# Loading and turning batch 0 by units of 192 tokens in a windowed attention with a gated feed-forward

## The chip, the cores and the metric

The kernel runs on one core of a Trainium2 chip. The metric is the device time of one execution in microseconds; the median of three runs before the change is 339.5 us (339.3 to 340.37). The core has a matrix engine (TensorE, PE in the profile; its weight loads are PEld), a vector engine (VectorE, DVE), a scalar engine (ScalarE, ACT), GpSimd (POOL) and SyncE (SP), which issues transfers. Transfers that change the type from float32 to float16 are issued from GpSimd here, plain ones from SyncE.

## What is computed

Causal attention with a window of 64 tokens over 8 batches, 8 heads, 576 tokens and 64 elements per head, then a gated feed-forward layer over the 4608 tokens.

```python
scores = q @ k.T / sqrt(64)                  # (8, 8, 576, 576)
mask = (rel >= 0) & (rel < 64)               # rel = query position - key position
attn = softmax(where(mask, scores, -1e9))
x = (attn @ v).transpose(0, 2, 1, 3).reshape(4608, 512)
out = (maximum(x @ w_gate, 0) * (x @ w_val)) @ w_out      # 512 -> 1536 -> 512
```

All inputs and the output are float32. The kernel calculates its matrix products in float16 with float32 sums.

## The kernel before

The attention works in 24 units of 192 tokens, three to a batch (U = 192, UB = 3). Two units make one tile of 384 tokens (TT) for the feed-forward layer, which has 12 tiles. The program is written as an interleaving: a small planner with a clock ("W") is given pieces of attention at planned times, and they are put into the instruction streams between the matmuls of the feed-forward layer. The clock orders the instructions; it makes no engine wait.

For a batch, k and q arrive with 18 tokens to a partition, four heads over 128 partitions, and VectorE turns them in blocks of 32, so that the head's elements lie on the partitions (32 partitions per head, two elements of float16 packed as one float32):

```python
def qk_load(b, name, hh):                    # from GpSimd, float32 -> float16
    tile_ = nat[b, name, hh] = a_in.tile([128, S // 32 * D], FP16, ...)
    src = (q if name == "q" else k)[b, G * hh:G * hh + G]
    nc.gpsimd.dma_start(tile_, src.rearrange("h (i j) d -> (h i) (j d)", i=32))

def k_first(hh):                             # batch 0 only: float32, from SyncE
    k32 = nat["k32", hh] = x_sb.tile([128, S // 32 * D], FP32, ...)
    nc.sync.dma_start(k32, k[0, G * hh:G * hh + G].rearrange(...))

def qk_trans(b, name, hh, j0=0, j1=S // 32):
    ...
    nc.vector.transpose(dst.rearrange("p (i j) -> p j i", i=32)[:, j0:j1], src[:, j0:j1])
```

A unit's values stand in a tile of 128 keys for each of its three windows of 64 queries. The upper 64 partitions are loaded, and the lower ones are copied from the upper ones of the window before by VectorE:

```python
def v_load(u):
    for w in range(UB):
        nc.gpsimd.dma_start(v16s[uu][64:128, w, :, 0:64], ...)

def v_low(u):
    if uu > 0:
        nc.vector.tensor_copy(v16s[uu][0:64, 0, :, 0:64], v16s[uu - 1][64:128, UB - 1, :, 0:64])
    nc.vector.tensor_copy(v16s[uu][0:64, 1:UB, :, 0:64], v16s[uu][64:128, 0:UB - 1, :, 0:64])
```

A unit then runs: scores (`u_st`, 48 matmuls with 32 rows each), exp on ScalarE (`u_exp`), mask by a product on VectorE (`u_mask`; units 0 and 1 instead add a bias before the scores by a matmul with the identity, `u_bias`), values and row sums (`u_pv`), copies of the values out of PSUM on ScalarE (`u_copy`), the row sums turned (`u_sum`), their reciprocal turned back (`u_back`) and the product (`u_norm`), which writes the tile `xt`. Units 0 and 1 have narrow value matmuls with the sums made by separate matmuls with ones; from unit 2 on a wide form gives values and sums at once, for which `v16s` holds columns of ones. `heat` is a row of matmuls on zeros, which do no part of the result.

The feed-forward layer takes a tile or a half of one (`hidden`: for each block of w_gate and w_val four matmuls, relu on ScalarE, gate product on VectorE) and then `output` with w_out. The start of the program, cut:

```python
for hh in range(2):
    k_first(hh)
for hh in range(2):
    qk_load(0, "q", hh)
...
heat(12, units[0]["st"][1][3])
bands(); constants(); v_ones(1, nc.vector)
for hh in range(2):
    for part in range(2):
        k_round(hh, part, 2)                 # float32 -> float16 on ScalarE
W.at(5.5, lambda: v_load(0)); W.at(5.6, lambda: v_load(1))
W.at(6.4, lambda: w_load(*G3[0], 13.7))      # w_gate, first third
W.at(6.5, lambda: w_load(*V3[0], 16.3))      # w_val, first third
...
W.at(21.0, lambda: v_ones(2, nc.vector)); W.at(21.0, lambda: v_ones(0, nc.vector))
plan_unit(2, 23.0, ...)
plan_unit(3, 42.15, *fast)
plan_unit(4, 49.3)
plan_unit(5, 56.95, *fast)
T = 67.0
...
W.advance(13.7)
ready(1)
hidden(0, 0, U, 0, 4, 4)                     # unit 0, first four blocks
ready(2)
hidden(0, U, TT, 0, 4, 4)                    # unit 1, first four blocks
hidden(0, 0, TT, 4, NF, 4)
output_by_rows(0)
ready(3)
hidden(1, 0, U)
output(1, (0,))
ready(4)
hidden(1, U, TT)
output(1, (1, 2))
for t in range(2, NU // 2):
    ready(2 * t + 2)
    hidden(t, 0, TT)
    (output if t < NU // 2 - 1 else output_last)(t)
```

`ready(n)` puts attention into the streams until n units are done; `w_load` loads a third of a weight matrix (512 KB as float16) from GpSimd. In the profile L419 is the gate and value matmul of `hidden`, L433 the output matmul, L407 the gate product, L356 `u_norm`, L311 the wide values, L289 and L296 the narrow values and sums, L249 the scores, L198 and L199 `v_low`.

Of the kernel before, what the change touches and what calls it, by code (L numbers as in the profile page):

```python
# [12 lines left out]
MUL = mybir.AluOpType.mult  # L13

# [28 lines left out]
def kernel(  # L43
# [10 lines left out]
    nc = tc.nc  # L54
# [32 lines left out]
    v16s = [persist.tile([128, UB, H, 128], FP16, name=f"v16_{i}") for i in range(UB)]  # L87
# [4 lines left out]
    ident = consts.tile([128, 128], FP16)  # L92

# [21 lines left out]
    def v_ones(i, eng):  # L115
        eng.memset(v16s[i][64 if i == 0 else 0:, 0, :, 64:128], 1.0)
        for w in range(1, UB):
            eng.memset(v16s[i][:, w, :, 64:128], 1.0)  # L118

    def k_zeros():  # L120
        nc.vector.memset(kTs[1][:, :, 0:64], 0.0)

    def constants():
        nc.vector.memset(kTs[0][:, :, 0:64], 0.0)
        nc.vector.memset(v16s[0][0:64, 0], 0.0)
        nc.vector.memset(ones, 1.0)
        nc.vector.memset(ones0, 1.0)
        nc.vector.memset(ones0[0:64], 0.0)

# [40 lines left out]
    def k_first(hh):  # L170

        k32 = nat["k32", hh] = x_sb.tile([128, S // 32 * D], FP32, name="k32", bufs=2)
        nc.sync.dma_start(k32, k[0, G * hh:G * hh + G].rearrange("h (i j) d -> (h i) (j d)", i=32))

    def k_round(hh, part, parts):
        n = S // 32 * D // parts
        if part == 0:
            nat[0, "k", hh] = a_in.tile([128, S // 32 * D], FP16, name=f"k{hh}", bufs=2)
        nc.scalar.copy(nat[0, "k", hh][:, n * part:n * part + n], nat["k32", hh][:, n * part:n * part + n])  # L179
# [8 lines left out]
    def v_load(u):  # L188
        b, uu = divmod(u, UB)
        for w in range(UB):  # L190
            k0 = U * uu + 64 * w
            nc.gpsimd.dma_start(v16s[uu][64:128, w, :, 0:64], v[b, :, k0:k0 + 64].rearrange("h p d -> p h d"))  # L192

    def v_low(u):

        uu = u % UB
        if uu > 0:
            nc.vector.tensor_copy(v16s[uu][0:64, 0, :, 0:64], v16s[uu - 1][64:128, UB - 1, :, 0:64])  # L198
        nc.vector.tensor_copy(v16s[uu][0:64, 1:UB, :, 0:64], v16s[uu][64:128, 0:UB - 1, :, 0:64])  # L199

    def u_bias(u, gs=range(G)):

        d = units.setdefault(u, {})
        if "st" not in d:
            st_tiles(u)
        d["biased"] = True
        for to in d["st"][0] + d["st"][1] if u == 0 else [d["st"][0][g] for g in gs]:
            n = 1 if u == 0 else 2
            nc.tensor.matmul(to[:, 0:n * U].rearrange("p (n c) -> p n c", c=64), ident,
                             bias[:, None, :].to_broadcast([128, n * UB, 64]),  # L210
                             start=True, stop=False, skip_group_check=True)
# [6 lines left out]
    def st_tiles(u):  # L218
        d = units.setdefault(u, {})
        one = lambda name: f_ps.tile([128, 512], FP32, name=name, tag="h")  # L220
        two = lambda name: a_ps.tile([128, 2, 512], FP32, name=name, tag="a")
        if u == 0:
            d["st"] = [[one("st") for _ in range(G)]]
            halves = [two("st") for _ in range(2)]
            d["st"].append([halves[g // 2][:, g % 2] for g in range(G)])
        elif u == 1:
            half = two("st")
            d["st"] = [[half[:, 0], half[:, 1], one("st"), one("st")]] * 2
        else:
            halves = [two("st") for _ in range(2)]  # L230
            d["st"] = [[halves[g // 2][:, g % 2] for g in range(G)]] * 2
        if u == 0:
            d["spare"] = d["st"][1][3][:, 256:512]
            d["st"] = [[x[:, 0:512 if hh == 1 and g == 3 else 256] for g, x in enumerate(row)] for hh, row in enumerate(d["st"])]

    def u_st(u, hhs=(0, 1)):
        d = units.setdefault(u, {})
        kT, qT = kTs[(u // UB) % 2], qTs[(u // UB) % 2]
        biased = "biased" in d
        if not biased:  # L240
            st_tiles(u)
        ks = U * (u % UB)
        for hh in hhs:
            for w in range(UB):
                c = U * (hh if u else 0) + 64 * w
                for dh in range(2):
                    for g in range(G):
                        rows = slice(32 * g, 32 * g + 32)
                        nc.tensor.matmul(  # L249
                            d["st"][hh][g][:, c:c + 64],  # L250
                            kT[rows, hh, ks + 64 * w:ks + 64 * w + 128, dh],
                            qT[rows, hh, ks + 64 * w:ks + 64 * w + 64, dh],
                            start=(dh == 0 and not biased), stop=(dh == 1),
                            skip_group_check=biased)
        d.setdefault("p", [None] * G)
        return 0.49

    def u_exp(u, g, hh=None):
        d = units[u]
        if not hh:  # L260
            d["p"][g] = a_p.tile([128, 2, U], FP16, name="p")
        if hh is None:
            nc.scalar.activation(d["p"][g].rearrange("p h c -> p (h c)"), d["st"][0][g][:, 0:2 * U], ACT.Exp, scale=scale)  # L263
        else:
            nc.scalar.activation(d["p"][g][:, hh], d["st"][hh][g][:, 0:U], ACT.Exp, scale=scale)
# [6 lines left out]
    def u_pv(u, cs=(0, 2, 1, 3)):  # L272
        if u > 1:
            return u_pv_wide(u)
        d = units[u]
        v16 = v16s[u % UB]
        if u == 0 and cs[0] == 0:
# [348 lines left out]
```

The softmax here doesn't subtract the row's maximum and nothing guards it: scores larger than these inputs give would overflow.

## Time and profile before

| | before |
|---|---|
| median of three runs | 339.5 us (339.3 to 340.37) |
| span of the profiled run | 337.9 us |
| TensorE busy | 325.5 us, 96% |
| VectorE busy | 260.3 us, 77% |
| ScalarE busy | 176.7 us, 52% |
| GpSimd busy, load issues included | 74.0 us, 22% |

A line of the timeline gives the start, the busy time, the engine, the line of the kernel, the operation, output and inputs with their shapes, how many instructions are merged in it, and in square brackets the idle time before it with what ended it. Busy time of TensorE includes `heat`, so the share at the start says nothing of useful work.

### The profile page before, as it was taken

How to read it: one execution, taken by the hardware profiler on the slowest of the kernel's cores; microseconds unless marked ns; L12 is line 12 of the kernel's file. 1: busy time of each engine (PE TensorE's matmuls, PEld its weight loads, DVE VectorE, ACT ScalarE, POOL GpSimd, SP SyncE). 2: the span in 40 equal slices, each digit the busy share in tenths (PEclk: the TensorE clock that was granted, in tenths of full speed). 3: DMA queues.
4: the chain of work that ended last, by engine and by line, in shares of the span. 5: the costliest groups of instructions: out<-in, count | busy, mean ns of one | idle time of the engine just before them, and what ended most of it. 6: DMA issues, size and time to landing. Idle time of an engine off the chain costs nothing.

```text
span 337.9 us, 8605 instructions
## 1 busy us (share of the span) xinstructions
PE 325.5 (96%) x3522; PEld 197.3 (58%) x3522; DVE 260.3 (77%) x493; ACT 176.7 (52%) x383; POOL 74.0 (22%) x121
## 2 busy tenths in 40 slices
PE   8699998999999999999999999999999999999995
PEld 4485485856546656655655655654655664664653
DVE  5878878998998874897989974888889874884430
ACT  4546165745636646645555564564564664653321
POOL 8724341250213221320210410150120200000000
PEclk9989999999999999999999999999999999999999
DMA  8999998496343933491242853296214402001002
GB/s 214 178 206 193 204 203 135 31 139 98 24 77 49 158 51 71 29 185 70 17 53 73 111 75 98 18 143 123 17 10 111 32 3 93 2 2 71 24 0 94
DMA packets 52886, 29.44 MB, mean 87 GB/s; under 512 B 39280, under 2 KB 44272, under 8 KB 52848
## 3 DMA queue, kind: packets, MB, share of 16 engines
q0 software_dynamic: 47088, 18.29, 47.4%
q1 hardware_dynamic: 5616, 10.55, 8.7%
q8 instruction: 27, 0.44, 0.6%
q14 instruction: 11, 0.09, 0.1%
q10 hardware_dynamic: 144, 0.07, 0.1%
HBM read 37.75 MB, written 9.44 MB: 140 GB/s over the span
## 4 chain that ended last, share of the span: by engine, by line
PE 81%; DVE 13%; issue 3%; DMA 2%; ACT 0%; DVEq 0%; ACTq 0%; POOLq 0%
PE h L419 52%; PE op L433 21%; PE pv L311 5%; PE st L249 3%; DVE sT L341 2%; DVE qT L186 2%; DMA q<-in_q_dram 2%; DVE g_sb L407 2%; DVE kT L186 1%; DVE xt L356 1%; DVE rs L350 1%; DVE p L270 1%; PE op L465 1%; DVE v L118 1%; DVE rT L348 0%
## 5 line engine op out<-in xcount | busy, mean ns | idle before, releaser
L419 PE MATMUL h<-xt,wg 128*128 128x384 f16 (+1 forms) x640 | 117.5, 313 | 1.7 <-DVE xt L356 1.7
L419 PE MATMUL h<-xt,wv 128*128 128x384 f16 (+1 forms) x640 | 116.7, 311 | 1.0 <-DVE g_sb L407 1.0
L407 DVE TENSOR_TENSOR g_sb<-r_sb,h 128x384 f16<-128x384 f32 x144 | 78.3, 550 | 48.8 <-PE h L419 47.1
L404 ACT ACTIVATE r_sb<-h 128x384 f32<-128x384 f32 x144 | 70.2, 492 | 67.0 <-PE h L419 55.3
L433 PE MATMUL op<-wo,g_sb 128*128 128x512 f16 x420 | 93.0, 379 | 0.0
L192 POOL DMA_DIRECT2D v<-in_v_dram x72 | 49.5, 696 | 181.0 <-PE pv L311 95.3
L419 PEld LDWEIGHTS <-wg 128*128 128x128 f16 x640 | 61.5, 99 | 36.5 <-DVE xt L356 1.6
L419 PEld LDWEIGHTS <-wv 128*128 128x128 f16 x640 | 59.0, 98 | 31.7 <-issue 1.3
L433 PEld LDWEIGHTS <-g_sb 128*128 128x128 f16 x420 | 40.3, 98 | 46.6
L341 DVE STREAM_TRANSPOSE sT<-pv 64x384 f32<-64x384 f32 x88 | 51.1, 580 | 9.7 <-PE pv L311 7.7
L329 ACT COPY xv<-pv 64x384 f32<-64x384 f32 x88 | 41.6, 473 | 21.5 <-DVE sT L341 8.1
L440 ACT COPY o_sb<-op 128x512 f32<-128x512 f32 x35 | 20.5, 586 | 54.6 <-PE op L433 54.6
L263 ACT ACTIVATE p<-st 128x384 f16<-128x384 f32 x92 | 39.7, 492 | 4.2 <-PE st L249 4.1
L270 DVE TENSOR_TENSOR p<-p,mask 128x384 f16<-128x384 f16 x88 | 27.5, 352 | 0.3 <-ACT p L263 0.2
L350 DVE STREAM_TRANSPOSE rs<-rT 128x768 f32<-128x768 f32 x24 | 23.5, 978 | 0.8
L356 DVE TENSOR_TENSOR xt<-xv,rs 128x768 f16<-128x768 f32 x24 | 22.8, 948 | 0.8
L311 PEld LDWEIGHTS <-v 128*128 128x128 f16 x528 | 18.6, 98 | 4.2 <-issue 0.8
L186 DVE STREAM_TRANSPOSE kT<-k 128x576 f32<-128x576 f32 (+1 forms) x18 | 19.7, 1121 | 1.4 <-ACT k L179 1.3
L311 PE MATMUL pv<-p,v 128*128 128x64 f16 x528 | 19.7, 193 | 1.1 <-DVE p L270 0.6
L186 DVE STREAM_TRANSPOSE qT<-q 128x576 f32<-128x576 f32 x16 | 18.9, 1239 | 1.1 <-DMA q<-in_q_dram 1.1
L249 PEld LDWEIGHTS <-kT 32*128 32x128 f16 x1152 | 11.0, 92 | 10.0 <-issue 9.9
L249 PE MATMUL st<-qT,kT 32*128 32x64 f16 x1152 | 13.9, 189 | 2.3 <-DVE qT L186 2.0
(47 smaller groups left out, 91.8 us busy)
## 6 DMA issues: line engine op xcount, KB each, us to landing
out_dram<-o_sb SPq DMA_DIRECT2D x35, 256.0 KB, 2.0
q<-in_q_dram POOLq DMA_DIRECT2D x16, 288.0 KB, 8.1
v<-in_v_dram POOLq DMA_DIRECT2D x72, 64.0 KB, 3.2
k<-in_k_dram POOLq DMA_DIRECT2D x14, 288.0 KB, 6.1
wg<-in_moe_w_gate_dram POOLq DMA_DIRECT2D x3, 512.0 KB, 10.1
wv<-in_moe_w_val_dram POOLq DMA_DIRECT2D x3, 512.0 KB, 11.9
wo<-in_moe_w_out_dram POOLq DMA_DIRECT2D x3, 512.0 KB, 13.7
k<-in_k_dram SPq DMA_DIRECT2D x2, 576.0 KB, 4.0
```

The source lines that it names most:

```text
L186: nc.vector.transpose(dst.rearrange("p (i j) -> p j i", i=32)[:, j0:j1], src[:, j0:j1])
L192: nc.gpsimd.dma_start(v16s[uu][64:128, w, :, 0:64], v[b, :, k0:k0 + 64].rearrange("h p d -> p h d"))
L249: nc.tensor.matmul(d["st"][hh][g][:, c:c + 64], kT[rows, hh, ks + 64 * w:ks + 64 * w + 128, dh], qT[rows, hh, ks + 64 * w:ks + 64 * w + 64 ...
L263: nc.scalar.activation(d["p"][g].rearrange("p h c -> p (h c)"), d["st"][0][g][:, 0:2 * U], ACT.Exp, scale=scale)
L270: nc.vector.tensor_tensor(p, p, mask[:, None, :].to_broadcast([128, 2 * UB, 64]), MUL)
L311: nc.tensor.matmul(d["pv"][c % 2][:, c // 2, e, 64 * w:64 * w + 64], v16[:, w, 128 * h - 64 * e:128 * h - 64 * e + 128], d["p"][h % G][:, ...
L329: nc.scalar.copy(d["xs"][rows, n::2], d["pv"][n][rows, :, e, 0:U])
L341: nc.vector.transpose(to[64 * e:64 * e + 64, half::2], d["pv"][half][64 - 64 * e:128 - 64 * e, :, e, 0:U])
L404: nc.scalar.activation(part(r_sb), part(h1), ACT.Relu)
L407: nc.vector.tensor_tensor(g_sb[:, f:f + w, c0:c1], part(r_sb), part(h2), MUL)
L419: nc.tensor.matmul(h[:, b * n:b * n + n], wt[:, c, (f + b) * 128:(f + b) * 128 + 128], xt[:, c, c0:c1], start=(c == 0), stop=(c == NC - 1))
L433: nc.tensor.matmul(op, g_sb[:, f, bass.ds(sub * 128, 128)], wo[:, f], start=(f == 0), stop=(f == NF - 1))
```

## The change

Batch 0 is treated by units of 192 tokens, and with all eight heads at once: k and q of a unit arrive with 12 tokens to a partition, those of unit 0 (and k of unit 1) in float32 over SyncE's queue. They are rounded, turned by TensorE with a permutation (`turn`) and copied out of PSUM. Every head then has its 64 elements on 64 partitions, so the scores of units 0 to 2 take 24 matmuls with 64 rows. Unit 2 gets the bias and the narrow values, too. Batch 1 is loaded and turned by units in the old way. v is loaded with 128 partitions for every second window, and the windows between are copied from it, for units 1 to 5 on GpSimd. The ones for the values are written by GpSimd. Unit 1's values come after unit 0's first gates in the streams, and the first half of tile 1 before the output of tile 0. The aim is to have the first x earlier and to take work off VectorE in the first tiles.

```diff
+    def all_rows(name, u):
+        src = (q if name == "q" else k)[0, :, U * u:U * u + U]
+        return src.rearrange("h (i j) d -> i h (j d)", j=JA)          # JA = 12
+    def all_load32(name, u, queue):
+        t32 = nat[name, u, 32] = a_in.tile([128, JA * D], FP32, ...)
+        queue.dma_start(t32, all_rows(name, u))
+    def all_round(name, u, copies):            # the columns shared among the engines in copies
+    def unit_flip(name, u):
+        for j in range(JA):
+            for hh in range(2):
+                nc.tensor.matmul(to[64 * hh:64 * hh + 64, 64 * j:64 * j + 64],
+                                 nat[name, u][:, D * j:D * j + D],
+                                 turn[:, G * hh:G * hh + G], start=True, stop=True, ...)
+    def unit_keep(name, u, cc, copy):          # PSUM -> qA or kA, half of the heads
-        for w in range(UB):
-            nc.gpsimd.dma_start(v16s[uu][64:128, w, :, 0:64], ...)
+        for g, lo, hi in parts or (((1, 0, 128), (3, 0, 128)), ((5, 0, 128),),
+                                   ((7, 0, 128), (NG - 1, 64, 128)))[uu]:
+            nc.gpsimd.dma_start(v16s[b % 2][lo:hi, g, :, 0:64], ...)
+    def v_spread(u, copy=None):                # nc.vector unless copy is given
@@ start of the program, cut
+        for name in "kq":
+            all_load32(name, 0, nc.sync)
+        heat(6, ...)
+        bands()
+        v_load(0, ((1, 0, 128), (3, 0, 64)))
+        all_load("q", 1)
+        v_load(1, ((3, 64, 128), (5, 0, 128)))
+        for wt, t in ((G3[0], 12.3), (V3[0], 14.9)):
+            w_load(*wt, t)
+        all_round("k", 0, (dve, act)); all_load32("k", 1, nc.sync); all_round("q", 0, (dve, act))
+        unit_flip("k", 0); u_bias(0); unit_flip("q", 0)
+        (unit_keep of k and q: one half on dve, one on act)
+        heat(6, ...); v_spread(0); u_st(0); (u_exp); heat(6, ...); u_pv(0)
+        (u_sum, u_copy, u_back, u_norm of unit 0)
+        all_round("k", 1, (pool,))
+        w_load(*G3[1], 17.5)
+        v_spread(1, pool)
+        heat(3, ...)
+        (unit_flip and unit_keep of k and q of unit 1, all keeps on act)
+        heat(4, ...); u_bias(1); u_st(1); (u_exp)
+        v_fixed(1, nc.gpsimd)                  # ones and zeros of the second v tile
+        (k, q, v of unit 2)
+        for wt, t in ((V3[1], 23.4), (G3[2], 26.0), (V3[2], 28.6)):
+            w_load(*wt, t)
+        (loads of units 3 to 5, w_out after unit 3's, v_spread(2..5, pool), v_fixed(0, nc.gpsimd))
+        narrow(1, 13.7, 13.9)                  # values, sums, norm of unit 1
+        (unit 2: flip at 20.6, scores at 22.0, narrow(2, 25.9, 27.4))
-        plan_unit(3, 42.15, *fast)
-        plan_unit(4, 49.3)
-        plan_unit(5, 56.95, *fast)
-        T = 67.0
+        for u, t in ((3, 37.0), (4, 46.0), (5, 54.0)):
+            plan_trans(u, t - 2.6)
+            plan_unit(u, t)
+        T = 67.5
-        W.advance(13.7)
+        W.advance(12.3)
         hidden(0, 0, TT, 4, NF, 4)
-        output_by_rows(0)
         ready(3)
         hidden(1, 0, U)
+        output_by_rows(0)
         output(1, (0,))
```

## The prediction

> **What bounds the kernel now**
>
> I read the page first, then the tables by stretch, then who waits for whom, then the start instruction by instruction, since the diff touches almost only the start.
>
> ```profile
> PE 325.5 (96%) x3522; PEld 197.3 (58%) x3522; DVE 260.3 (77%) x493; ACT 176.7 (52%) x383; POOL 74.0 (22%) x121
> PEclk9989999999999999999999999999999999999999
> DMA  8999998496343933491242853296214402001002
> ```
>
> TensorE is the bound: 96% busy. The DMA row says that loads matter only in the first six slices (some 50 us). So a change in the loads and in batch 0 can win only what TensorE loses before the steady state, not a share of the whole.
>
> ```profile
> PE h L419 <- DVE xt L356: 1.7, 2, 1.2
> PE pv L289 <- ACT p L263: 1.3, 2, 1.1
> PE h L419 <- DVE g_sb L407: 0.7, 1, 0.7
> ```
>
> These are TensorE's waits in the first 75 us (total, times, longest). They are small, because before 17 us much of its busy time is warm-up matmuls on zeros. The time itself is in the order of events:
>
> ```profile
> 13.36 0.65 DVE L338 STREAM_TRANSPOSE sT<-pv 128x192 f32<-128x192 f32 x2 [0.61 <-ACT xv L325]
> 13.93 0.28 DVE L198 COPY v<-v 64x512 f16<-64x512 f16 x1
> 14.13 0.41 DVE L199 COPY v<-v 64x1024 f16<-64x1024 f16 x1
> 14.57 0.30 DVE L348 RECIPROCAL rT<-sT 128x24 f32<-128x24 f32 x1
> 14.91 0.98 DVE L350 STREAM_TRANSPOSE rs<-rT 128x768 f32<-128x768 f32 x1
> 15.99 0.96 DVE L356 TENSOR_TENSOR xt<-xv,rs 128x768 f16<-128x768 f32 x1
> 17.00 2.72 PE L419 MATMUL h<-xt,wg 128*128 128x192 f16 x16 [0.53 <-DVE xt L356]
> 19.50 0.96 DVE L356 TENSOR_TENSOR xt<-xv,rs 128x768 f16<-128x768 f32 x1
> ```
>
> Unit 0's normalised x is ready at 16.95 and the first gate matmul starts at 17.00; unit 1's x is ready at 20.46. Unit 1's value copies (13.93 to 14.54) lie right in unit 0's chain. The chain of waits goes further back, to the q load, which ends at 7.47.
>
> ```profile
> 15.00:16.00 1.00, 0.66 (x19) 0.46 (x20) 0.90 (x2) 0.91 (x3) 0.68 (x1) 1.00 1.18 196
> 18.00:19.00 1.00, 1.00 (x8) 0.92 (x7) 0.93 (x3) 1.00 (x4) 0.69 (x1) 0.50 1.23 203
> 20.00:21.00 1.00, 1.00 (x14) 1.00 (x12) 0.72 (x2) 0.25 (x1) 0.18 (x1) 0.95 1.28 221
> ```
>
> Columns: stretch, its length, then busy time and count of PE, PEld, DVE, ACT, POOL, then the granted clock, DMA share, GB/s. The first gates ran at half clock for about 3.4 us.
>
> ```profile
> 24.64 0.48 DVE L116 MEMSET v<- 128x512 f16 x1
> 25.18 1.02 DVE L118 MEMSET v<- 128x512 f16 x2
> ...
> 57.25 0.94 DVE L356 TENSOR_TENSOR xt<-xv,rs 128x768 f16<-128x768 f32 x1
> ```
>
> ```profile
> 58.24 1.49 PE h L419 x16
> ```
>
> ```profile
> 15.31 0.68 POOL L192 DMA_DIRECT2D v<-in_v_dram  x1 [0.48 <-DMA wg<-in_moe_w_gate_dram]
> 18.31 0.76 POOL L151 DMA_DIRECT2D wo<-in_moe_w_out_dram  x1 [2.33 <-DMA wv<-in_moe_w_val_dram]
> 20.82 0.75 POOL L151 DMA_DIRECT2D wo<-in_moe_w_out_dram  x1 [1.74 <-DMA wg<-in_moe_w_gate_dram]
> ```
>
> From VectorE's timeline, the chain and GpSimd's timeline: VectorE carries memsets between the gates and is late with unit 3's x, which opens the second feed-forward half only at 58.24. GpSimd's waits show when weights landed: the first gate block near 15.3, the first value block near 18.3, the next near 20.8, so 2.6 us each.
>
> I cut the span in three. **A**: to the first gate, 17.00. **B**: from there to tile 2's first gate at 74.77, 57.8 us. **C**: the rest, 263.1 us, which the change hardly touches. If TensorE never stopped in B it would do two tiles at 15.60 us for 96 gate and value matmuls and 7.77 for 36 output matmuls (both in the chain), 46.7, and four attention units at 0.48 + 0.70, 4.7: together 51.4. B loses 6.4: about 1.6 by the half clock, the rest by waits for VectorE and by matmuls that miss their best spacing.
>
> **What the Trainium skill says**
>
> "TensorE: Matmul & The Clock Gate", Part 1 (the clock gate): after a window of about 3.4 us without enough work the clock halves, and comes back after a busy one. The trace agrees with the length (half clock from about 16.8 to 20.2), though the window before it was some 45% busy, not idle.
> "DMA: Bandwidth & Descriptors", Issuing engines are not separate DMA queues: all issuers share the same 16 engines. The trace agrees: after 3 us the DMA share stays above 0.99 although SyncE and GpSimd issue. A hardware queue thus gains only by order and by fewer bytes ahead.
> "GPSIMD Engine Reference", Engine selection: one-input operations run at roughly line rate there. No run here shows it yet: before has no GpSimd copy.
> "TensorEngine Tiling (Array Packing)", Key Properties: tiles work in parallel. The trace agrees: six 64-column value matmuls in two column halves start within 0.10 us, 17 ns each.
>
> **The change part by part**
>
> *Loads ahead of unit 0.* Before: k of the whole batch, 1.18 MB in float32, and q, 0.59 MB after the cast. After: k and q of 192 tokens, 0.39 MB each. The 1-us table shows 396 and 406 GB/s at 3 to 5 us, and k's first half, issued at 0.81, is used at 4.39: 3.6 us, of which 0.59 MB take 1.5 and 2.1 are latency. 0.39 MB take 1.0, so k is there at 0.81 + 2.1 + 1.0 = 3.9 and q at 4.9. Before, q landed at 7.47 and its second half later.
>
> *Turning.* Removed: six transposes on VectorE, 0.72 to 1.26 us each. Added per name: two rounding copies of 384 columns side by side on VectorE and ScalarE (ScalarE's 576 cost 0.66, so about 0.47), 24 turning matmuls (17 ns each warm, 0.4 us; 1.0 if cold), and two copies out of PSUM of 384 columns, about 0.5 each (ScalarE's 384-column activation: 0.49), side by side. q: 4.9 + 0.5 + bias of k's tiles in between + 0.7 + 0.5 = about 7.5.
>
> *Unit 0.* Scores 24 matmuls 0.4, four exps at 0.41 (four took 1.65), values behind the exps: 7.5 + 0.4 + 1.65 + 0.6 = 10.2. Then two pairs of sum transposes (0.65 a pair), the first pair hidden: 10.9. Reciprocal 0.30, broadcast 0.98, norm 0.96 with their gaps: 13.2. The value copies on VectorE wait for v, near 8.5, and are done before the exps end.
>
> *First weights.* Ahead of them stood k, q and six v loads of 64 KB, 2.16 MB; now it is two k loads and a q load in float32 (1.18), q of unit 1 (0.20) and v (0.38): 0.4 MB less, at about 200 GB/s 2 us: gates near 13.3, values near 15.9. Unit 1's turning, bias and scores now stand before unit 0's gates in TensorE's order; ScalarE has to make four copies out (about 2.0) after unit 0's copies (11.3), and scores end near 13.7. So **A ends at 13.7**, 3.3 us earlier.
>
> *Unit 1.* Its exps take ScalarE from 13.8 to 15.4, its values end at 15.9, sums 16.6, back and norm 2.3: x at 18.9, 1.6 before the old 20.46. TensorE has one block for unit 0 in between, so it waits some 1.6 us there.
>
> *B afterwards.* Work: 46.7, units 3 to 5 3.5, unit 2 in the narrow form 2.5 (two turns 0.8, bias 0.65, scores 0.35, values 0.75), unit 1's values 0.75: 53.5. Losses: 1.6 for unit 1's x; half of a cold window, 0.8; VectorE in tile 1's stretch, 2.0. For the last: it keeps 12 masks at 0.34, 12 sum transposes at 0.59, three times 2.24 of back and norm, 12 short transposes at about 0.47 and 24 gates at 0.54: 36.5 us, beside about 35 us of TensorE's work, so it stays full, although memsets (3.0) and value copies (four units at 0.7) have gone to GpSimd. Sum: 57.9, as long as before. B gains nothing: it takes over 2.1 us more work and loses 2.0 less.
>
> *C.* Same schedule, value copies of the same volume, fewer v loads: 0.
>
> Sum: 13.7 + 57.9 + 263.1 = 334.7 for the span, 3.2 less. Against that the new weight order (unit 2's k, q and v, 0.6 MB, 3 us, between the second gate block and the second value block) may bare up to 1 us, and GpSimd's copies stand between its load issues: I put 0.3 against it. 339.5 - 3.2 + 0.3 = **336.6 us**.
>
> **Rivals**
>
> *Weights become the bound.* The second value block would land near 24.1; TensorE needs it near 24 to 26. Before, the last value block landed near 28.6 and was consumed by 36.3, a reserve of some 5 us, which speaks against. If GpSimd waits for v between its issues, each block slips 2 to 3 us: time 338 to 341.
>
> *VectorE is relieved enough that B runs clean.* For: the memsets and copies are gone from 24 to 36 us and unit 3 is planned 5 us earlier. Against: the 36.5 us just counted. Time about 334.
>
> *The start does not move.* If TensorE is cold in its small matmuls, or unit 1's chain on ScalarE holds unit 0's gates in TensorE's order, the first gate comes at 15.5 or later and unit 1's x no earlier than 20.5. Then the 2.1 us of added work are bare: 339 to 341.
>
> **Range and chances**
>
> The first of these gains reaches 334, the bad cases 341; the middle is 336.6. I give 333.6 to 340.0 eight times in ten. Faster by over 2% means under 332.7: that needs A down by 4 and B by 3 together: 0.06. Slower by over 2%, over 346.3, needs stalls that nothing in the trace suggests: 0.03. Within 2%: 0.91.
>
> **What would show it**
>
> In the changed profile: the first gate matmul near 13.7 (over 15: the start's sum is wrong); unit 1's x near 18.9 with a TensorE wait for it of 1 to 2 us; V blocks not among the waits; one cold window or none after the first gate; tile 2's first gate near 71.6; C at 263 within 0.5. It is wrong if C changes, or if the wait for weights or for GpSimd's copies exceeds 2 us.

## Result and profile after the change

| | before | after |
|---|---|---|
| median of four runs | 339.4 us (339.14 to 340.37) | 341.44 us (341.26 to 341.82) |
| ratio after / before, 95% interval | | 1.0056 [1.0035, 1.0078] |
| span of the profiled run | 337.9 us | 340.1 us |
| A, to the first gate | 17.00 | 16.98 |
| B, to tile 2's first gate | 57.8 | 59.2 (16.98 to 76.18) |
| C, the rest | 263.1 | 263.9 |

The kernel became 0.6% slower; 336.6 us had been predicted. A did not move at all, although it was to gain 3.3 us, and B, which was to stay at 57.9, grew by 1.4.

The page of the kernel after, first the engines' busy times, then the granted clock and the transfers' share in 40 slices:

```profile
PE 326.5 (96%) x3593; PEld 197.5 (58%) x3593; DVE 250.2 (74%) x484; ACT 177.4 (52%) x387; POOL 79.6 (23%) x116
...
PEclk9999999999999999999999999999999999999999
DMA  9999998599975931279323922244002002002002
```

VectorE got rid of 10.1 us, and the time gained nothing by it: TensorE is still 96% busy. The half-clock stretch of 17 to 20 us (0.50 before) is gone in this execution, and still the time is longer. So the loss has to be looked for in the order of events. TensorE's waits in the first 79 us (total, times, longest):

```profile
PE h L487 <- DVE xt L423: 1.9, 1, 1.9
...
PE st L318 <- DVE qT L243: 1.2, 2, 0.6
...
PE kf L224 <- POOL ka L214: 0.6, 1, 0.6
```

In the kernel after, L487 is the gate and value matmul, L423 the norm that writes x, L224 the turning, L235 the keeping, L305 the new scores, L318 the old ones, L357 the narrow values, L405 the sum transposes, L214 the rounding, L501 the output matmul. The timeline of all engines, cut to the two units' chains:

```profile
5.04 0.36 DVE L214 CAST ka<-k 128x384 f16<-128x384 f32 x1 [2.50 <-DMA k<-in_k_dram]
...
5.58 0.54 SPq L208 DMA_DIRECT2D k<-in_k_dram  x1
...
6.77 0.36 DVE L214 CAST qa<-q 128x384 f16<-128x384 f32 x1 [1.36 <-DMA q<-in_q_dram]
...
12.73 0.82 POOL L214 CAST ka<-k 128x768 f16<-128x768 f32 x1 [5.15 <-DMA k<-in_k_dram]
...
13.61 0.57 PE L224 MATMUL kf<-turn,ka 128*64 128x64 f16 x24 [0.60 <-POOL ka L214]
...
14.38 1.33 DVE L423 TENSOR_TENSOR xt<-xv,rs 128x768 f16<-128x768 f32 x1
...
14.96 1.22 POOL L267 COPY v<-v 64x512 f16<-64x512 f16 x1
14.96 0.88 ACT L235 CAST qA<-qf 128x384 f16<-128x384 f32 x2
...
16.13 2.01 POOL L124 MEMSET v<- 128x2304 f32 x1
...
16.52 0.52 PE L305 MATMUL st<-qA,kA 64*128 64x64 f16 x24
...
16.98 1.49 PE L487 MATMUL h<-xt,wg 128*128 128x192 f16 x16
...
18.40 0.28 PE L357 MATMUL pv<-p,v 128*64 128x64 f16 x6
...
18.99 1.18 DVE L405 STREAM_TRANSPOSE sT<-pv 128x192 f32<-128x192 f32 x4 [3.28 <-PE pv L363]
...
21.62 0.96 DVE L423 TENSOR_TENSOR xt<-xv,rs 128x768 f16<-128x768 f32 x1
...
22.63 1.48 PE L487 MATMUL h<-xt,wg 128*128 128x192 f16 x16 [1.90 <-DVE xt L423]
```

Read it once for each unit. For unit 0: k is used at 5.04 and q at 6.77, and x is ready at 14.38 + 1.33 = 15.71. TensorE is free to open the gates then, but unit 1's bias and scores stand before them in its order, and they end at 16.98. The first gate weights would not have allowed much more: their load was issued at 6.04 and landed 9.7 us later, near 15.7. For unit 1: its k was issued at 5.58 and used at 12.73, its turning follows at 13.61, its values come only at 18.40, behind unit 0's gates, and its x is ready at 22.58, where before it was ready at 20.46. TensorE sits idle for 1.90 us.

### The profile page after: what moved, and what is told of

The parts are those of the page before. It is cut to its first block, busy times and chain, and to the rows that moved or that the text cites. A ratio compares the mean times of both kernels' runs of the same rounds, so it can differ in the third digit from the quotient of the medians.

```text
span 340.1 us, 8701 instructions
## 1 busy us (share of the span) xinstructions
PE 326.5 (96%) x3593; PEld 197.5 (58%) x3593; DVE 250.2 (74%) x484; ACT 177.4 (52%) x387; POOL 79.6 (23%) x116
## 4 chain that ended last, share of the span: by engine, by line
PE 82%; DVE 11%; issue 3%; POOL 2%; ACT 1%; DVEq 0%; ACTq 0%; POOLq 0%
PE h L487 52%; PE op L501 20%; PE pv L378 4%; DVE sT L408 3%; PE st L318 3%; DVE qT L250 2%; DVE rs L417 1%; DVE xt L423 1%; POOL v L256 1%; PE op L533 1%; DVE kT L250 1%; DVE g_sb L475 1%; DVE kT L243 0%; DVE qT L243 0%; PE st L275 0%
## 5 line engine op out<-in xcount | busy, mean ns | idle before, releaser
L487 PE MATMUL h<-xt,wg 128*128 128x384 f16 (+1 forms) x640 | 116.4, 310 | 1.9 <-DVE xt L423 1.9
L487 PE MATMUL h<-xt,wv 128*128 128x384 f16 (+1 forms) x640 | 116.4, 310 | 0.1
L472 ACT ACTIVATE r_sb<-h 128x384 f32<-128x384 f32 x144 | 69.8, 493 | 67.4 <-PE h L487 59.2
L501 PE MATMUL op<-wo,g_sb 128*128 128x512 f16 x420 | 93.1, 379 | 0.0
L487 PEld LDWEIGHTS <-wg 128*128 128x128 f16 x640 | 60.5, 98 | 36.3 <-issue 2.1
L487 PEld LDWEIGHTS <-wv 128*128 128x128 f16 x640 | 58.6, 98 | 30.8 <-issue 0.3
L501 PEld LDWEIGHTS <-g_sb 128*128 128x128 f16 x420 | 40.3, 98 | 46.3
L256 POOL DMA_DIRECT2D v<-in_v_dram x41 | 34.7, 851 | 115.1 <-PE pv L378 77.7
L408 DVE STREAM_TRANSPOSE sT<-pv 64x384 f32<-64x384 f32 x84 | 48.8, 581 | 9.8 <-PE pv L378 7.9
L396 ACT COPY xv<-pv 64x384 f32<-64x384 f32 x84 | 39.6, 472 | 19.8 <-DVE sT L408 7.9
L328 ACT ACTIVATE p<-st 128x384 f16<-128x384 f32 x96 | 41.5, 491 | 7.1 <-PE st L318 5.8
L338 DVE TENSOR_TENSOR p<-p,mask 128x384 f16<-128x384 f16 x84 | 26.3, 351 | 1.4 <-ACT p L328 1.2
L423 DVE TENSOR_TENSOR xt<-xv,rs 128x768 f16<-128x768 f32 x24 | 23.1, 962 | 1.2 <-DVE rs L417 0.5
L378 PE MATMUL pv<-p,v 128*128 128x64 f16 x504 | 18.5, 193 | 0.3 <-DVE p L338 0.3
L318 PEld LDWEIGHTS <-kT 32*128 32x128 f16 x1008 | 9.8, 92 | 9.4 <-issue 8.7
L318 PE MATMUL st<-qT,kT 32*128 32x64 f16 x1008 | 12.5, 189 | 2.6 <-DVE qT L250 1.4
L250 DVE STREAM_TRANSPOSE kT<-k 128x576 f32<-128x576 f32 x12 | 14.7, 1239 | 0.2
L250 DVE STREAM_TRANSPOSE qT<-q 128x576 f32<-128x576 f32 x12 | 14.0, 1234 | 0.0
```

The source lines that it names most:

```text
L256: nc.gpsimd.dma_start(v16s[b % 2][lo:hi, g, :, 0:64], v[b, :, 64 * g - 64 + lo:64 * g - 64 + hi].rearrange("h p d -> p h d"))
L318: nc.tensor.matmul(d["st"][g][:, c:c + 64], kT[rows, hh, ks + 64 * w:ks + 64 * w + 128, dh], qT[rows, hh, ks + 64 * w:ks + 64 * w + 64, dh ...
L378: nc.tensor.matmul(d["pv"][c % 2][:, c // 2, e, 64 * w:64 * w + 64], v16[:, w, 128 * h - 64 * e:128 * h - 64 * e + 128], p_of(u, h)[:, 64 ...
L396: nc.scalar.copy(d["xs"][rows, n::2], d["pv"][n][rows, :, e, 0:U])
L408: nc.vector.transpose(to[64 * e:64 * e + 64, half::2], d["pv"][half][64 - 64 * e:128 - 64 * e, :, e, 0:U])
L472: nc.scalar.activation(part(r_sb), part(h1), ACT.Relu)
```

## Experiments

Four reasons seemed possible for the late start. Theory 1: unit 1's k comes late, since one float32 buffer serves k of both units and SyncE could issue the second load only after the first k was rounded (it waited 3.3 us). Theory 2: the casting loads that GpSimd issues at the same time slow k and q of unit 0. Theory 3: TensorE is slow in unit 0's turning, as at half clock (the turning of k took 0.85 us in this execution and 0.57 in e1; the clock column of the table by stretch shows 1.00 there all the same). Theory 4: the order is at fault, since unit 1's work stands in front of unit 0's gates, and behind other work on the way to its own x. Each ratio below is to the kernel before, with runs of the same chip, and its 95% interval.

**One more buffer for k** (`e1_k_buffer`)

```diff
-        t32 = nat[name, u, 32] = a_in.tile([128, JA * D], FP32, name=f"{name}32", bufs=1)
+        t32 = nat[name, u, 32] = a_in.tile([128, JA * D], FP32, name=f"{name}32", bufs=2)
```

> The changed kernel with one thing altered: k and q in float32 get two buffers each, so that the load of unit 1's k no longer waits on SyncE for unit 0's k to be rounded (it was issued at 5.58 us and used at 12.73). Theory 1 (unit 1's late k sets the start): k is there by 7 to 9 us, GpSimd rounds it then, the gates start when unit 0's x is ready, near 15.7 instead of 16.98, unit 1's x is ready near 19.5 to 20.5 instead of 22.58, TensorE's wait of 1.9 us for it is gone, and the time is 2 to 3 us less, near 339. Rival 2 (the 16 transfer engines are the bound, so an earlier k only delays something else): unit 0's q or the v loads come later by as much and the time stays within 0.7 us of 341.4.

341.11 us, ratio 1.0066 [1.0051, 1.0081]: no gain. Unit 1's k was issued at 2.15 and rounded at 8.83, some 4 us earlier. The timeline of this kernel, TensorE:

```profile
12.96 0.57 PE L224 MATMUL kf<-turn,ka 128*64 128x64 f16 x24
...
16.33 1.49 PE L487 MATMUL h<-xt,wg 128*128 128x192 f16 x16
...
21.99 1.48 PE L487 MATMUL h<-xt,wg 128*128 128x192 f16 x16 [1.90 <-DVE xt L423]
```

The turning moved by 0.65 us and waits for nothing now: it simply stands behind unit 0's values. Those came hardly sooner (11.10 instead of 11.33), though unit 0's exps ended 0.85 us earlier, because they now had to wait for v. VectorE's timeline of this kernel has its first copy of v, which stood at 9.12 in the changed kernel, at

```profile
10.62 0.42 DVE L265 COPY v<-v 64x1024 f16<-64x1024 f16 x1 [2.39 <-DMA v<-in_v_dram]
```

So part of what the earlier k gained was paid with a later v, as rival 2 of the expectation had it. The idle time of 1.90 is the same to the hundredth. Theory 1 falls as the main cause; the second buffer is needed again in `e5_turn_early`.

**Unit 0's gates ahead of unit 1's scores** (`e2_gates_first`)

```diff
-        u_bias(1); u_st(1)
-        for c in order: u_exp(1, c)
+        W.at(13.2, lambda: u_bias(1)); W.at(13.3, lambda: u_st(1))
+        for c in order: W.at(13.4, lambda c=c: u_exp(1, c))
```

> The changed kernel with the bias, scores and exps of unit 1 put behind unit 0's first gates in the streams. Rival 1 (the order in TensorE holds the first gates): the gates start at 15.75 instead of 16.98 and the time falls by about 1.2 us. Theory 1 (unit 1's x is what TensorE waits for): the gates start at 15.75, but unit 1's x is later by about 1 us, near 23.6, the wait for it grows from 1.9 to 4 us, and the time is 0.5 to 1.5 us more than 341.4.

342.3 us, 1.0102 [1.0085, 1.0119]: slower. TensorE's timeline of this kernel:

```profile
15.68 1.16 PE L487 MATMUL h<-xt,wg 128*128 128x192 f16 x12 [0.32 <-DMA wg<-in_moe_w_gate_dram]
```

The gates did begin at 15.68, and what they waited for last was their weights, for 0.32 us; x had been ready at 15.53. But unit 1's x came at 23.48 instead of 22.58, and TensorE again waited 1.73 us for it. An earlier first gate is worth nothing where the second unit's x sets the pace.

**Casting loads of unit 0 and 1 later** (`e3_late_v`): the memsets of the second v tile are put ahead of them on GpSimd, so that nothing competes with k and q.

```diff
         bands()
+        v_fixed(1, nc.gpsimd)
         v_load(0, ((1, 0, 128), (3, 0, 64)))
 ...
-        v_fixed(1, nc.gpsimd)                 # behind unit 1's exps
```

> The changed kernel with GpSimd's 2.5 us of constant writes for the second value tile moved from behind unit 1's exps to ahead of the first v load, so that the casting loads start at about 4.9 instead of 2.3 us. Theory 2 (the casting loads slow unit 0's k and q): k is used near 4.1 instead of 5.04, q near 5.1 instead of 6.77, unit 0's x comes 1 to 1.5 us earlier. If unit 1's late k sets the end all the same, the time moves by less than 0.7 us unless k of unit 1 comes earlier, too. Against theory 2: k and q are used within 0.2 us of before.

342.32 us, 1.0101 [1.0086, 1.0116]; v itself is late now, so the time says nothing of theory 2, but the landing does. Tables by stretch (stretch, length, busy time and count of the five engines, clock, share and GB/s of the transfers) and VectorE's timeline of this kernel:

```profile
4.50:5.00 0.50, 0.00 (x0) 0.00 (x0) 0.08 (x1) 0.09 (x1) 0.50 (x2) 1.00 0.79 215
5.00:5.50 0.50, 0.17 (x6) 0.17 (x8) 0.28 (x1) 0.43 (x1) 0.50 (x1) 1.00 0.29 74
5.50:6.00 0.50, 0.50 (x24) 0.50 (x22) 0.00 (x0) 0.00 (x0) 0.50 (x2) 1.00 0.00 0
```

```profile
4.92 0.36 DVE L214 CAST ka<-k 128x384 f16<-128x384 f32 x1 [0.61 <-DMA k<-in_k_dram]
6.30 0.39 DVE L214 CAST qa<-q 128x384 f16<-128x384 f32 x1 [1.02 <-DMA q<-in_q_dram]
```

With no casting load beside them k was used only 0.12 us earlier than in the changed kernel and q 0.47. Even that is hardly an effect of the loads: in the other kernels that leave the casting loads where they were, q is used between 6.30 (e1, the same as here) and 7.06 (e4). So theory 2 falls, and 1.4 us of q's delay against the predicted 4.9 is its own: 1.0 of it has already come with k (3.9 predicted), and q follows k by 1.4 instead of 1.0. The transfers begin at 2.25 and end at about 5.3 us, so the 0.79 MB of k and q moved at some 260 GB/s on the whole, though the stretch from 3.5 to 4.0 shows 381. q was usable 1.0 us after the last byte. The Trainium skill, "DMA: Bandwidth & Descriptors", Anatomy of one DMA, says for GpSimd's path that most of a transfer's fixed cost lies behind the last byte, which must be confirmed before the semaphore moves; this stretch of 1.0 us without any transfer agrees, on SyncE's queue.

**TensorE kept busy before the turning** (`e4_heat9`)

```diff
-        heat(6, units[0]["st"][3])
+        heat(9, units[0]["st"][3])
```

> The changed kernel with 9 instead of 6 warm-up matmuls at the start, so that TensorE stays busy up to unit 0's k. Theory 3 (TensorE is at half clock in unit 0's turning): the 24 turning matmuls take 0.55 instead of 0.85 us, the bias 0.8 instead of 1.46, and unit 0's x is 0.7 to 1.0 us earlier; the time changes by less than 0.5 us, since unit 1's k is still late. If the time falls by 0.7 or more, unit 1's x is not the bound.

341.5 us, 1.0077 [1.0058, 1.0095]. The turning took 0.57 and the bias 0.82 instead of 1.46, and unit 0's x came 0.5 us earlier, at 15.23, though 0.37 of that is the norm (0.96 us: here it began before the GpSimd copy that it met, and it was the copy that took longer, 0.98 instead of 0.61), and q landed 0.3 later. But unit 1's k was rounded at 13.15, 0.4 later, and the gates began at 17.40. No gain: again unit 1's scores stand in front.

**Unit 1 turned ahead of unit 0's values** (`e5_turn_early`, with e1's buffer)

```diff
-        heat(6, flipped["k", 0][:, 1])
+        heat(3, flipped["k", 0][:, 1])
+        all_round("k", 1, (pool,))
+        (unit_flip and unit_keep of k and q of unit 1, moved here; heat before and behind them dropped)
         u_pv(0)
```

> The kernel with two k buffers, and in it unit 1's turning and its copies out of PSUM put ahead of unit 0's values (in place of warm-up matmuls), where TensorE and ScalarE sat waiting for v. Theory 4 (unit 1's x is late because its chain of turning, four copies, bias, scores and exps begins only after unit 0's values, not because its k lands late): the scores of unit 1 end near 13.5 instead of 16.4, the gates start with unit 0's x near 15.5, unit 1's x is ready near 20.9 instead of 21.94, and the time is 0.8 to 1.4 us under that of the kernel with two k buffers (341.1). Rival 2 (transfers are the bound: first gate weights landed at 15.6, first value weights at 18.0): the scores end as early, but the start of unit 1's gates stays within 0.4 us of 21.99 and the time within 0.4.

340.51 us, 1.0054 [1.003, 1.0079]. Its timeline, TensorE and the norms:

```profile
13.53 0.52 PE L305 MATMUL st<-qA,kA 64*128 64x64 f16 x24
...
14.64 0.96 DVE L423 TENSOR_TENSOR xt<-xv,rs 128x768 f16<-128x768 f32 x1
...
15.65 1.48 PE L487 MATMUL h<-xt,wg 128*128 128x192 f16 x16 [1.59 <-DVE xt L423]
...
21.29 1.48 PE L487 MATMUL h<-xt,wg 128*128 128x192 f16 x16 [1.90 <-DVE xt L423]
```

Unit 1's scores now end at 14.0, 3 us earlier, and TensorE waits 1.59 us for unit 0's x. Yet unit 1's values still stand behind those gates, and from there the chain to its x takes what it took: the wait of 1.90 is back. What is left of the earlier start is 1.3 us at tile 2's first gate (74.84 instead of 76.18; e1 has 75.53). The ratio shows none of it; the executions fall in two groups, three at 340.4 to 340.5 and two near 341.9, and these two have a mean clock of 0.994 to 0.995 instead of 0.999 to 1.0, as much as one half-clock stretch of 3.4 us would make (estimate: half of 3.4 us over 339). So early turning by itself is worth about 1 us or nothing. It also rests on e1's buffer: with one buffer unit 1's k is rounded only from 12.73 on.

**Values ahead of the gates, with and without early turning** (`e6_values_first` is e5 and this line; `e9_values_first_only` is the changed kernel and this line alone)

```diff
-        narrow(1, 13.7, 13.9)
+        narrow(1, 11.0, 11.2)
```

> The kernel before this one in the list, with unit 1's values and sums put ahead of unit 0's first gates instead of behind them. Theory 4: values near 14.5 to 15.4, unit 1's x near 18.9, TensorE goes from unit 0's values block (weights at 18.0) to unit 1's gates at 19.3 with no wait for x, and the time is 1.3 to 2 us under the kernel before it, near 338.5 and 0.1 to 0.3% faster than the kernel before the change. Rival 2: the later weights are the bound, TensorE waits for the second value block instead (it starts no earlier than 29 us), and the time falls by less than 0.5.

> The changed kernel with one thing altered: unit 1's values and sums ahead of unit 0's first gates. With late turning, unit 1's exps end at 18.55 us, so its values can end near 18.7 instead of 19.15 and its x is ready about 0.5 us earlier, while the gates start 1.7 us later. Theory 4 (unit 1's x is what TensorE waits for, and its chain begins too late): 0 to 0.6 us less than 341.4. If the placing of the values behind the gates were itself the loss, the gain would be 1.3 us as in the pair of kernels with early turning.

e6: 339.21 us, 0.9991 [0.9978, 1.0004]. e9: 341.41 us, 1.005 [1.0035, 1.0065]. The timeline of e6:

```profile
13.51 0.52 PE L305 MATMUL st<-qA,kA 64*128 64x64 f16 x24
...
14.62 0.96 DVE L423 TENSOR_TENSOR xt<-xv,rs 128x768 f16<-128x768 f32 x1
...
16.62 1.49 PE L487 MATMUL h<-xt,wg 128*128 128x192 f16 x16
...
18.84 0.96 DVE L423 TENSOR_TENSOR xt<-xv,rs 128x768 f16<-128x768 f32 x1
...
19.85 1.50 PE L487 MATMUL h<-xt,wg 128*128 128x192 f16 x16 [0.38 <-DVE xt L423]
```

And of e9:

```profile
16.32 0.52 PE L305 MATMUL st<-qA,kA 64*128 64x64 f16 x24
...
18.88 1.49 PE L487 MATMUL h<-xt,wg 128*128 128x192 f16 x16
...
22.10 1.49 PE L487 MATMUL h<-xt,wg 128*128 128x192 f16 x16 [0.41 <-DVE xt L423]
```

This is the main finding. Values first with late turning gives nothing: it pushes the first gates to 18.88. Early turning alone leaves the wait of 1.90. Together they bring unit 1's x to 19.80 and the first gates to 16.62, 2.8 and 0.4 us earlier than in the changed kernel, and tile 2's first gate from 76.18 (74.84 in e5) to 73.43. By the ratios e6 is 0.6%, some 2.1 us, under e5; by the medians it is 1.3. The slowdown by the change is undone; the gain that was predicted is not there. What else keeps A at 16.62 was not tested: TensorE waits 1.6 us for unit 1's exps before its values, and the gate weights land near 15.9 in any case. Values first with e1's buffer but with late turning was not run either.

**Memsets behind the weight issues** (`e7_consts_late`: e6, and `v_fixed(1, nc.gpsimd)` moved behind the three `w_load`)

> As the kernel before it in the list, with GpSimd's 2.5 us of constant writes moved behind the issue of the last gate and value weights. Theory 5 (GpSimd's other work delays the load issues, and the weights now bind): the second value block starts 1 to 2 us earlier and the time falls by 0.8 us or more. Theory 4 alone (weights have a reserve of a microsecond): within 0.5 us.

The reason to try it is a hole in the changed kernel's transfers, by stretches of 1 us:

```profile
18.00:19.00 1.00, 1.00 (x34) 0.84 (x33) 0.01 (x1) 1.00 (x4) 0.87 (x3) 1.00 1.19 204
19.00:20.00 1.00, 1.00 (x24) 0.91 (x17) 1.00 (x4) 0.59 (x3) 0.97 (x3) 1.00 0.20 31
```

GpSimd spends 16.13 to 18.7 on memsets before it issues the next loads, so the rate falls to 31 GB/s. 339.49 us, 1.0003 [0.9991, 1.0016], against 0.9991 for e6 in the same set: the hole costs nothing that shows.

**Units 4 and 5 turned earlier** (`e8_turns_earlier`: e7 and)

```diff
-            plan_trans(u, t - 2.6)
+            plan_trans(u, t - (2.6 if u == 3 else 5.6))
```

> As the kernel before it in the list, with the turning of units 4 and 5 on VectorE planned 3 us earlier. In the changed kernel TensorE waits 0.62 and 0.55 us in their scores for the second half of this turning. If only its place in VectorE's order is at fault, both waits go and the time falls by about 1 us. If VectorE is full there (36.5 us of work counted in the prediction), the waits move to unit 3's or 4's x or to the gates and the time moves by less than 0.4 us.

338.67 us (338.01 to 339.38), 0.9972 [0.9962, 0.9983], by the ratios 0.3% or 1.1 us under e7, by the medians 0.8. TensorE's two waits for `qT` (1.2 us in the changed kernel) are gone. Part of the difference lies in the clock: six of e7's twelve executions and three of e8's have a mean of 0.993 to 0.995. Without these the medians are 338.87 and 338.53. So the earlier turns are worth 0.3 to 1.1 us. This kernel is faster than the changed one and, by 0.3%, than the one before.

**Value copies of units 1 to 5 back on VectorE** (`e10_v_on_vector`, from the changed kernel)

```diff
-        v_spread(1, pool)
+        v_spread(1)
-        v_spread(2, pool) ...
+        for u, t in ((2, 23.0), (3, 38.4), (4, 47.4), (5, 55.4)):
+            W.at(t, lambda u=u: v_spread(u))
```

> The changed kernel with the value copies of units 1 to 5 on VectorE instead of GpSimd, placed as before the change (1.4 us after the scores' planned time; unit 1's behind unit 0's norm). VectorE gets some 3 us more work up to 70 us. If VectorE is full in tile 1's stretch, as the prediction had it, the time rises by 1 us or more. If VectorE has room (it sat idle for 5.3 us in one piece near 27 in the changed kernel), the time stays within 0.6 us of 341.4, and GpSimd's copies bought nothing here; GpSimd then issues the loads earlier.

342.85 us, 1.0096 [1.0075, 1.0116], 1.4 us over the changed kernel. The start did not suffer (first gates and waits alike); the loss is at 60 to 69 us, seen in the timeline of this kernel:

```profile
64.32 0.59 ACT L508 COPY o_sb<-op 128x512 f32<-128x512 f32 x1 [3.71 <-DMA out_dram<-o_sb]
...
64.95 0.82 PE L487 MATMUL h<-xt,wv 128*128 128x192 f16 x8 [0.87 <-ACT o_sb L508]
```

ScalarE's copy of the output waited 3.71 us for a transfer that frees its buffer (1.78 in the changed kernel), and TensorE waited for ScalarE. Without copies GpSimd issues its loads earlier, and the output transfers then lie beside more of them; that this is the reason was not tested by itself. So having the copies on GpSimd is worth 1.4 us here. That it is so by what the copies shift, and not by VectorE's time, is argued from this wait and not shown.

**Unit 2 turned and scored in the old way** (`e11_unit2_old_way`: e8, with k and q of unit 2 turned by VectorE and the wide values, as units 3 to 5; GpSimd's constant writes are placed anew, too)

> The fastest kernel so far (two k buffers, early turning, values first, constants late, turns of units 4 and 5 earlier: 338.7) with unit 2 in the old way: k of its 192 and the 64 tokens before and q loaded in the old layout, turned on VectorE, no bias, mask by product, wide values. TensorE then does 0.48 + 0.71 instead of about 3.0 us for unit 2 (two turns 0.88, bias 0.9 with its wait, scores 0.46, values 0.83). Theory 6 (the new way of unit 2 costs TensorE 1.8 us that nothing hides): 1.2 to 1.9 us less, near 337. Rival: VectorE is late with unit 2's x because of four turns, four masks and wider sums, TensorE waits for it, and the gain is under 0.5 us.

340.24 us, 1.0012 [0.9997, 1.0027], slower than e8, although TensorE has 1.9 us less to do (1.2 instead of 3.1 for unit 2). Its timeline (line numbers are shifted, L504 is the gate and value matmul):

```profile
27.76 2.77 PE L504 MATMUL h<-xt,wv 128*128 128x384 f16 x16 [2.27 <-DMA wv<-in_moe_w_val_dram]
```

What was saved is waited for: the second value block was issued at 17.98 and is used at 27.76. The weights have become the bound here, and what the narrow unit 2 costs by itself stays open.

**All small repairs together** (`e12_combined`: e11, nine `heat`, four more on an idle tile behind unit 1's exps, one of unit 1's keeps on VectorE)

> The kernel before it in the list with TensorE kept at full clock: 9 instead of 6 warm-up matmuls at the start, four in the idle time before unit 1's values, and one of unit 1's four copies out of PSUM on VectorE. In the profile of the kernel with earlier turns, a half-clock window of 3.4 us lay on the first gates and cost 1.6 us; the two kernels before it in their list had none in their profiled runs. If such windows come in some executions only, the median falls by 0.3 to 1 us and the spread of the times gets smaller; if warm-up matmuls make no difference, it stays within 0.3 us.

339.74 us, 1.0008 [0.9988, 1.0028]. The wait for the second value block stays at 2.13 us, and the clock falls to 0.50 in the 2 us from 30 on; the block behind the wait takes 4.10 us instead of the 2.77 in e11. In this execution the wait is paid twice; e11's profiled execution has the same wait and no half clock behind it.

**The value block issued ahead of unit 2's k, q and v** (`e13_weights_ahead`: e11 with unit 2's turns planned 1.6 us and its scores 1.2 us later, and)

```diff
+        w_load(*V3[1], 20.1)
         tail_load(); v_load(2)                # k, q and v of unit 2
-        for wt, t in ((V3[1], 23.4), (G3[2], 26.0), ...
+        for wt, t in ((G3[2], 26.0), ...
```

> The kernel with unit 2 in the old way, with the second value weights issued ahead of unit 2's k, q and v, and unit 2's turns planned 1.6 and its scores 1.2 us later. If their place in the load order was the bound, the wait of 2.3 us for them goes, no other of the same size comes, the last gate and value weights have a reserve, and the time falls by 1.5 to 2.5 us from 340.2[...]. If the transfer rate is the bound (178 GB/s over the first 40 us here against 200 before the change), the wait moves to the third gate weights or to unit 2's turns, and the gain is under 1 us.

341.66 us, 1.0065 [1.0039, 1.0091]. TensorE's waits in its first 79 us:

```profile
PE h L504 <- DVE xt L440: 2.2, 1, 2.2
...
PE h L504 <- DMA wg<-in_moe_w_gate_dram: 1.4, 1, 1.4
...
PE st L335 <- DVE qT L208: 0.9, 1, 0.9
```

The wait for the value block is gone, and 4.5 us of other waits stand in its place: for unit 2's x, which comes late with its loads and its turns, for the third gate block and for `qT`. That fits the rate of the transfers as the bound: over the first 40 us this kernel moves 172 GB/s, e11 178, the changed kernel 169 and the kernel before 200. What lowers the rate was not tested.

**A warm clock for e8** (`e14_idle_heat`: e8 and four `heat` on an idle tile behind unit 1's exps)

> The kernel with earlier turns of units 4 and 5 (338.67 us, 338.0 to 339.4; unit 2 in the new way), with four warm-up matmuls in TensorE's idle time before unit 1's values. If a half-clock window of 3.4 us that falls on the first gates in some executions makes the spread, the profile has no such window, the times draw together and the median falls by 0.3 to 0.8 us. If the windows come whatever TensorE does there, median and spread stay within 0.2 us.

338.56 us (337.85 to 339.98), 0.9978 [0.9961, 0.9995]. e8's profiled execution shows a half clock in its first gates and this one does not; tables by stretch, e8 first:

```profile
17.00:18.00 1.00, 1.00 (x8) 0.95 (x7) 0.93 (x4) 0.54 (x2) 1.00 (x2) 0.50 1.26 210
```

```profile
17.00:18.00 1.00, 1.00 (x14) 0.85 (x12) 0.93 (x4) 1.00 (x5) 0.83 (x2) 1.00 1.23 206
```

By the ratio it does not differ from e8. All its twelve executions have a mean clock of at least 0.998, so none had the half-clock stretch, and the spread is no smaller. So the half clock is not all that spreads e8's times; what else does stays open.

## Why the prediction was wrong

**Time.** 336.6 was predicted and 341.44 measured, above the range. The span was to be 334.7 and is 340.1: 5.4 us, of which A has 3.3, B 1.3 and C 0.8.

**A: the step that failed.** The first gate was to come at 13.7 and came at 16.98. Along the prediction's own terms:

| term | predicted | measured | difference |
|---|---|---|---|
| q landed (measured: used) | 4.9 | 6.77 | 1.9 |
| q landed to q turned | 2.6 | 2.83 (to 9.60) | 0.2 |
| turned to unit 0's values | 2.7 | 2.59 (to 12.19) | -0.1 |
| values to unit 0's x | 3.0 | 3.52 (to 15.71) | 0.5 |
| x to first gate, behind unit 1's scores | 0.5 | 1.27 (to 16.98) | 0.8 |

The largest single error is "0.39 MB take 1.0, so k is there at 3.9 and q at 4.9". The rate of 396 to 406 GB/s came from the middle of 1.18 MB with 18 tokens (4.6 KB) a partition, and was taken for the whole load. The new loads have 12 tokens (3 KB), and e3 shows what they need with nothing beside them: k used at 4.92, q at 6.30, some 260 GB/s with the ramp and 381 at best. The competition that a reader would suspect first is at most the other 0.5, and the spread of the other kernels covers that. Why the average is so low was not tested; the smaller pieces are a guess. Of the 0.5 in the tail, 0.37 is the norm beside a GpSimd copy, 1.33 instead of 0.96. The slow turning was allowed for in the sum ("1.0 if cold") and unimportant: its removal (e4) gained nothing.

A second term failed and is hidden in this table, because something later came on top of it: "gates near 13.3" for the first weights. Their load was issued 2 us earlier than before (6.04 instead of 8.10), as the bytes ahead of it had let expect, but took 9.7 us instead of 6.9 and landed at 15.7. With everything else as predicted the first gate could not have come before that: of the 3.3 us at most 1.3 were to be had. Why the load took longer was not tested. The small remark that the window before the half clock was "some 45% busy" is a little low: TensorE's time from 13.27 to 16.68 is 51% busy.

**A and B: unit 1.** "Scores end near 13.7" was 3.3 us off, and this is what made the whole change a loss. The prediction put unit 1's turning where its data would be ready and did not read where it stands in TensorE's and ScalarE's order: behind unit 0's values and copies. With the data there 4 us earlier the turning moved by only 0.65 us (e1, where a later v took part of the gain); with the order altered on top, the scores end at 14.0 (e5), in spite of the late q. So the late scores are a matter of the order, once the second buffer is there. It also took the order "values behind gates" as given, with 1.6 us of wait; e6 shows that this wait (1.9 measured) was avoidable, and that taking it away without pushing the first gates back (18.88 in e9) needs early turning as well: with both, unit 1's x comes at 19.80 instead of 22.58 (18.9 predicted) and the loss is gone.

**B.** Its work was counted well: 46.7 for two tiles, 3.5 for units 3 to 5, 3.1 for unit 2 and 0.84 for unit 1's values, together 54.1 against 53.5. Lost were 5.1 instead of 4.4: 1.9 for unit 1's x, 1.2 in two waits for `qT`, some 2.0 in small gaps. The half clock, put at 0.8, did not show. The 2.0 for a full VectorE, of which 1.2 came, was wrong in kind: e8 removes the `qT` waits by turning earlier, so VectorE was late by order and not by load; it even sat idle for 5.31 us before 31.40.

**C.** 263.9 against 263.1: no change of schedule; 0.5 of it is the last output transfer, which ends 4.15 us after the last matmul instead of 3.62, and 0.3 a wait for `qT` at 82.15.

**Rivals.** The third, "the start does not move", said 339 to 341 and named both of its reasons, the cold small matmuls and unit 1's chain in front of unit 0's gates; the second of them is what e5 and e6 bear out. It should have had the main weight. "Weights become the bound" was wrong for the changed kernel, where TensorE never waits for a weight block, and is right for the next step (e11 to e13). But its figure was off here already: the second value block, "near 24.1", landed at 29.3 and was used at 30.47, so it was in time only because TensorE was late as well. "B runs clean" did not happen, though VectorE was relieved as counted.

## What to carry to other kernels

When work of a second unit is moved between pieces of the first, walk each engine's instruction order, not the times at which data are there: an engine does what stands next, and an early load or a free engine gains nothing behind it. Two halves of one repair can be worth more together than apart: here values first measured as zero and early turning as 1 us or less, and both together undo the whole loss, so a null result of one alone does not clear it. Before taking work off an engine, see whether the stage waits for that engine's load or for its order, and whether the transfers can follow: here 1.9 us of saved TensorE work turned into 2.3 us of waiting for weights.

## What was unexpected of the hardware

- Loads of 0.39 MB on SyncE's queue with 3 KB a partition were usable 4.1 us (k) and 4.8 us (q) after their issue with nothing beside them; 0.59 MB with 4.6 KB had taken 3.6. In the changed kernel unit 1's k, a load of the same size issued at 5.58 behind casting loads, took 7.1 us.
- Where a GpSimd copy of 512 columns (0.61 us alone) and VectorE's norm (0.96 alone) met, the one that began second took longer in all four kernels in which they met at the start: the norm 1.33 in the changed kernel, where the copy had begun 0.09 before it (and the next copy, begun inside the norm, 1.22), and the copy 1.42 in e2, 0.98 in e4 and 0.93 in e9, where the norm kept its 0.96. The Trainium skill, "GPSIMD Engine Reference", Specifications, says that GpSimd shares its SBUF interfaces with VectorE, and that instructions with two SBUF inputs contend; this agrees.
- GpSimd copies 512 columns of float16 in 0.61 us and 1024 in 1.04, where VectorE takes 0.29 and 0.42: twice as long or more, and 0.43 us for the second 512 columns against 0.13. The prediction had no trace for such copies.
- Over the first 40 us the changed kernel moved 169 GB/s where the old one had 200, though the engines that carry the transfers were kept as busy (share 1.30 in both tables).
